# The 96 rows of v around each block, interleaved over the partitions, in a kernel of three stages

## The chip, the cores and the metric

The kernel runs on one core of a Trainium2 chip. The time is device microseconds of one execution from start to end; a median of several executions is given, and the rows come from one profiled execution. Engines are PE (TensorE: matmuls and transposes), DVE (VectorE), ACT (ScalarE), POOL (GpSimd) and SP, whose queue issues nearly all the transfers. PEld is PE's loading of weights, which runs beside its matmuls.

## What is computed

Three stages follow each other, on 2 batches of 768 positions: an attention of 8 heads of 64 in a local window with summary keys, a convolution that gates a product, and a spatial gate. Every input comes as 64-bit floats.

```python
k_sum = k.reshape(B, H, nb, 32, D).max(axis=3)          # 24 summary keys
v_sum = v.reshape(B, H, nb, 32, D).mean(axis=3)
mask_l = np.abs(pos[:, None] - pos[None, :]) < 16       # local window
a = softmax(concat([where(mask_l, q @ k.T / 8, -1e9), q @ k_sum.T / 8 + log(32)]))
x = (a @ concat([v, v_sum]))                            # heads side by side: 768 x 512
gate = sigmoid(causal 5-tap convolution of x);  x = (gate * (x @ w_val)) @ w_out
h = relu(x @ w_in);  u, v = halves of h;  v_n = normalise v over its 512 columns
y = (u * (w_spatial @ v_n + b_spatial)) @ w_out2
```

## The kernel before, in words

The kernel first records every operation, and a class `Planner` then puts them in an order for each engine (`plan`): it keeps a clock for each engine, takes the durations from `cost`, and among the operations that could start picks the one of highest priority. `issue` (line 229; 230 after) hands them to the engines, so that nearly all rows of the profile bear this one line, and the names of tiles and the shapes tell them apart. Priorities come from the string `ORDER`: it lists pieces ("lk" loads one pair's k, "lq" q, "lv" v; "kw" builds the key window; "score", "at" and "pv" are the scores of one tick, their transposes and the product with v; "wout", "in1", "in0", "wval" load a 128-row tile of a weight; "wp" is part of the product of w_out and w_in; "vsum" and "put" are the mean of v; "gate", "val0", "u0" and so on are the later stages). A piece that needs another steps that one first.

The batches and heads form 8 pairs of heads, and 16 ticks of scores (half a sequence of one pair each). The sequence is cut into 12 blocks of 64. For each block the keys that count are 96 rows (the 64 of the block, 16 to the left and 16 to the right, the "halos") and 24 summary rows: 120 in all, which is the partition dimension of the pv product. For v these are partitions 0 to 119 of a tile `VW` of 1536 elements (two heads, 12 blocks, 64 columns), loaded by `load_v`: the 64 block rows into partitions 32 to 95, the left and right halos into the even and odd partitions of 0 to 31, from the neighbouring columns of the same array. Those are three transfers of 384, 96 and 96 KB for each pair. `put_vsum` puts the means into partitions 96 to 119 (a transfer at_u<-at_u for four pairs, and a POOL copy for each).

The keys stand in the same order along the free dimension of `KWT` (built by `windows`: an ACT copy "kev" of the block rows, POOL copies "halo" and "ksum"), and `load_masks` builds the additive mask in that order on POOL, once. In `scores` PE multiplies q with the key window (64x120 matmuls), DVE adds the mask and takes the maximum, ACT takes the exponential, POOL divides. `a_T` transposes on PE (128x128, with the identity in `moves`), and `pv` multiplies (120x64). ACT then splits x into a high part and a rest (`xl`), and the 128x384 matmuls of the later stages can begin.

Weights come as pairs of 32-bit words; `load64` makes one float of them with one ACT and two DVE operations. `w_product` multiplies the two weights between the stages (32 matmuls of 128x512). "hot" is a 128x264 filler matmul on `moves`. The SP queue is one list of transfers in the planned order.

Of the kernel before, what the change touches and what calls it, by code (L numbers as in the profile page):

```python
# [12 lines left out]
ALU = mybir.AluOpType  # L13
# [29 lines left out]
LOOK = {"PE": 0, "ACT": 0, "DVE": 0, "POOL": 100, "SP": 200}  # L43

ORDER = """
    mask hot*2 mask hot in1 wout*2 in1 lk*2 in1 kw hot lq hot wout score hot in1 lk kw wp*2 lq in0*2 wout kw lq
    score lk wp kw wp in0*2 vsum score wval lv lq at cw vsum at lv put score pv wval put lv wp score lv wp at score
    put*2 score wval lq pv score at wval wp hot lk pv at wv wp pv gate val0 at lq wu at pv kw val0 at wu lv wu
    val0*2 wu score wv pv lq lk pv kw pv lk lq score u0 lv u0 lk vsum gate val0 kw val0*3 u0 lv kw wv*2 vsum at put
    score put score*2 lv score*3 u0 put v0*3 at*3 put pv*4 at v0 f0 at ws at u0 v0 at pv*3 gate pv v0 u0 gate val1*2  # L50
    ws val1*4 f0 v1*2 s0 f0 val1*2 v1 s0 v1 u1 f0 f1 v1 s0 v1 u1 f1 u1 ws s0 s1 u1 f0*2 ws s0*2 s1 f1*3 s1 u0 ws*2
    u0 u1 ws s0 s1 s0 s1*2 u1*2 out2*2 u1 f0 s1 out2 s0*3 s1 s0 out2 r*2 s0*2 s1 f1 s1*2 r f1 r*3 s1 r s1 r*2 s1 r*3
"""

WIN = 10240 / 3
# [9 lines left out]
class Planner:  # L65
# [94 lines left out]
    def cost(o, eng, method, args, kw, ins, outs):  # L160
# [14 lines left out]
        if method == "dma_start":  # L175
            run = 4 * min(outs[0].ap[-1][1], ins[0].ap[-1][1]) if ins else 512
            total = 4 * size(outs[0]) * outs[0].ap[0][1]
            parts = outs[0].ap[0][1]
            o.rate = next(k for k in range(16, 0, -1) if parts % k == 0)
            rate = 130 if run <= 512 else 405 if parts > 96 else 235 if parts > 64 else 260 if parts > 16 else 150  # L180
            return (600 if eng == "POOL" else 980 if parts < 32 and run <= 512 else 840 if len(outs[0].ap) > 2 else 600 if parts == 64 else 410), None, total / rate, False
        if eng == "ACT":
            ptr = sum(1 for k in ("bias", "scale") if hasattr(kw.get(k), "ap")) + (method == "mul" and hasattr(args[2], "ap"))
# [265 lines left out]
def tile_kernel(ctx, tc, q, k, v, vn, w_val, conv_w, w_out, w_in, w_sp, b_sp, w_out2, mask_l, mask_r, eye, out):  # L449
# [4 lines left out]
    NB = S // QB  # L454
# [76 lines left out]
    def load_masks():  # L531
        pool.memset(moves, 0.0)
        pool.affine_select(out=moves, in_=moves, pattern=[[-1, 264]], compare_op=ALU.not_equal, fill=1.0, base=112, channel_multiplier=1)
        yield

        a3 = [x.rearrange("p (i c) -> p i c", c=KW) for x in added]
        pool.memset(a3[0][:, :, :WK], 0.0)
        pool.memset(a3[0][:, :, WK:], 27.725887222397812)
        for c in range(2):
            x = a3[0][64 * c : 64 * c + 64]  # L540

            for y, n, key in ((x[:, :, 32:WK], QB, 0), (x[:, :, 0:32:2], 16, -16), (x[:, :, 1:32:2], 16, QB)):
# [72 lines left out]
    def windows(n):  # L615

        need("lk", n + 1)
        kp = KT_[n]
        kw = KWT[n] = unit(F32)[:, : NB * KW].rearrange("p (j c) -> p j c", c=KW)
        km = smalls([P, 1, NS], "km", f"km{n}")  # L620
        dve.tensor_reduce(km[:, 0], kp.rearrange("p (m r) -> p m r", r=32), axis=AX.X, op=ALU.max)
        copy("kev", kw[:, :, 32:WK], kp.rearrange("p (j r) -> p j r", r=QB))

        pool.memset(bass.AP(kw.tensor, kw.offset, [kw.ap[0], [(NB - 1) * KW + 1, 2], [2, 16]]), 0.0)
        for x, y, m, dx, dy in ((QB - 16, KW, NB - 2, [80, 2], [1, 2]), (QB, 1, 2, [(NB - 2) * QB - 16, 1], [(NB - 1) * KW - 1, 1])):
            src = bass.AP(kp.tensor, kp.offset + x, [kp.ap[0], [QB if m > 2 else dx[0], m], dx, [1, 16]])
# [747 lines left out]
```

## Time and profile before

| what | us |
|---|---|
| median of 3 runs | 264.13 (263.94 to 265.03) |
| the profiled execution: its time | 265.06 |
| its span, first to last instruction | 263.3 |
| PE busy | 253.2 (96%) |
| PE weight loads busy | 217.5 (83%) |
| DVE busy | 189.4 (72%) |
| POOL busy | 163.7 (62%) |
| ACT busy | 158.9 (60%) |
| moved by DMA | 31.80 MB, mean 121 GB/s |

The shares are means over the span. The stages differ: the weights, q, k and v come in during the first 60 us, and the products fill the rest.

### The profile page before, as it was taken

The numbers are of one execution on the slowest core, as the hardware profiler recorded it, in microseconds if no ns is written. First come the engines' busy times: TensorE is split into PE (matmuls) and PEld (weight loads), VectorE is DVE, ScalarE is ACT, GpSimd is POOL, SyncE is SP. The second block draws the span as 40 slices with busy tenths as digits, with TensorE's granted clock in tenths as the row PEclk, the third lists the DMA queues.
The fourth block names the chain that finished last, engine by engine and source line by source line (L and its number), as shares of the span: only waits on it lengthen the run. The fifth ranks groups of instructions, "written<-read, shape, count | busy, mean of one in ns | idle before, by whom it ended". The sixth has DMA issues, their size and how long they took to land.

```text
span 263.3 us, 5380 instructions
## 1 busy us (share of the span) xinstructions
PE 253.2 (96%) x1878; PEld 217.5 (83%) x1878; DVE 189.4 (72%) x558; ACT 158.9 (60%) x440; POOL 163.7 (62%) x189
## 2 busy tenths in 40 slices
PE   7799999889999999999999999999999999999995
PEld 5255557459999998988998988999999998888884
DVE  1777969689999997799998687969734485650110
ACT  2578797999998699987453143314647443253222
POOL 7224444799797918991468354526999978863110
PEclk9999999999999999999999999999999999999999
DMA  6999999899730202700000000000000800014213
GB/s 219 404 402 410 312 301 236 238 313 343 258 110 0 92 4 94 276 0 2 2 1 1 0 2 0 0 0 2 1 1 2 319 0 2 0 76 163 80 42 120
DMA packets 10651, 31.80 MB, mean 121 GB/s; under 512 B 1520, under 2 KB 1984, under 8 KB 10624
## 3 DMA queue, kind: packets, MB, share of 16 engines
q1 hardware_dynamic: 10592, 31.43, 35.2%
q8 instruction: 15, 0.25, 0.4%
q14 instruction: 12, 0.10, 0.1%
q0 software_dynamic: 32, 0.02, 0.0%
HBM read 28.20 MB, written 3.15 MB: 119 GB/s over the span
## 4 chain that ended last, share of the span: by engine, by line
PE 75%; DMA 15%; ACT 6%; DVE 2%; SPq 1%; issue 0%; ACTq 0%; DVEq 0%
PE at_ps L229 75%; DMA at_u<-in_moe_w_val_dram 8%; ACT at_u L229 5%; DMA at_u<-in_moe_w_in_dram 4%; DMA at_u<-in_k_dram 3%; DVE at_u L229 1%; ACT at_ps L229 1%; SPq L229 1%; DVE sm L229 0%; ACT xl L229 0%; ACTq L229 0%; DVEq L229 0%
## 5 line engine op out<-in xcount | busy, mean ns | idle before, releaser
L229 PE MATMUL at_ps<-at_u,at_u 128*128 128x384 f32 (+4 forms) x1760 | 234.5, 321 | 3.5 <-DVE at_u L229 1.7
L229 PEld LDWEIGHTS at_ps<-at_u,at_u 128*128 128x128 f32 (+2 forms) x1760 | 201.2, 187 | 33.4 <-issue 14.0
L229 POOL TENSOR_TENSOR at_u<-at_u,at_u 128x384 fp32r<-128x384 f32 (+2 forms) x83 | 103.7, 1271 | 50.5 <-ACT at_u L229 50.0
L229 ACT CAST at_u<-at_u 128x384 fp32r<-128x384 f32 (+2 forms) x83 | 46.4, 593 | 44.0 <-DVE at_u L229 35.4
L229 DVE TENSOR_TENSOR at_u<-at_ps,at_u 128x384 f32<-128x384 f32 (+1 forms) x36 | 19.8, 553 | 36.1 <-PE at_ps L229 34.3
L229 ACT COPY at_u<-at_ps 120x384 f32<-120x384 f32 (+3 forms) x61 | 28.4, 503 | 22.5 <-PE at_ps L229 22.3
L229 ACT ACTIVATE at_u<-at_u,nm 128x120 f32<-128x120 f32 x96 | 36.6, 387 | 2.6 <-DVE nm L229 2.5
L229 POOL TENSOR_TENSOR at_u<-at_u,sm 128x360 f32<-128x360 f32 x32 | 25.6, 827 | 17.3 <-DVE sm L229 12.2
L229 DVE SCALAR_TENSOR_TENSOR at_u<-at_ps,cw,at_u 128x384 f32<-128x384 f32 (+3 forms) x64 | 36.4, 605 | 0.0
L229 DVE CUSTOM_DVE_ANT_0 at_u<-at_ps,mask 128x120 f32<-128x120 f32 x96 | 21.7, 273 | 2.9 <-PE at_ps L229 2.9
L229 ACT ACTIVATE at_ps<-at_u 128x512 f32<-128x512 f32 x20 | 12.9, 647 | 13.6 <-DMA at_u<-in_moe_w_out_dram 6.6
L229 DVE TENSOR_TENSOR at_u<-at_u,at_u 128x256 f32<-128x256 f32 (+2 forms) x25 | 19.1, 769 | 1.5 <-DMA at_u<-in_vn_dram 1.4
L229 ACT ACTIVATE at_u<-at_ps 128x512 f32<-128x512 f32 x20 | 11.5, 598 | 14.1 <-PE at_ps L229 14.1
L229 POOL COPY at_u<-at_u 128x320 f32<-128x320 f32 (+2 forms) x24 | 17.8, 751 | 1.4 <-DMA at_u<-at_u 0.7
L229 ACT ACTIVATION_READ_ACCUMULATOR at_u<-at_u,nm 128x1 f32 x96 | 18.5, 192 | 0.0
L229 DVE TENSOR_TENSOR at_u<-at_u 128x384 f32<-128x384 f32 (+5 forms) x31 | 15.4, 498 | 2.6 <-PE at_ps L229 2.4
L229 DVE TENSOR_SCALAR at_u<-at_u 128x512 uint32<-128x512 uint32 (+1 forms) x21 | 12.2, 581 | 5.4 <-DMA at_u<-in_moe_w_in_dram 5.4
L229 DVE SCALAR_TENSOR_TENSOR at_u<-at_ps,at_u 128x512 uint32<-128x512 uint32 x20 | 13.8, 689 | 2.2 <-ACT at_ps L229 1.1
L229 PE MATMUL at_ps<-moves,at_u 128*120 128x128 f32 x96 | 13.3, 275 | 0.9 <-POOL at_u L229 0.9
L229 PEld LDWEIGHTS at_ps<-moves,at_u 128*120 128x120 f32 x96 | 11.0, 137 | 3.2 <-POOL at_u L229 1.1
L229 DVE SCALAR_TENSOR_TENSOR at_u<-at_u,at_u 128x384 f32<-128x384 f32 x16 | 12.3, 790 | 0.1
L229 POOL TENSOR_TENSOR va<-va,power 128x1 f32<-128x1 f32 x12 | 8.0, 677 | 5.8 <-DVE va L229 5.6
(38 smaller groups left out, 128.4 us busy)
## 6 DMA issues: line engine op xcount, KB each, us to landing
at_u<-in_moe_w_in_dram SPq DMA_DIRECT2D x8, 512.0 KB, 9.0
at_u<-in_moe_w_out_dram SPq DMA_DIRECT2D x8, 512.0 KB
at_u<-in_k_dram SPq DMA_DIRECT2D x8, 384.0 KB, 7.7
at_u<-in_q_dram SPq DMA_DIRECT2D x8, 384.0 KB
at_u<-in_vn_dram SPq DMA_DIRECT2D x6, 512.0 KB, 9.6
at_u<-in_v_dram SPq DMA_DIRECT2D x8, 384.0 KB, 10.7
out_dram<-at_u SPq DMA_DIRECT2D x11, 256.0 KB, 2.0
at_u<-in_moe_w_spatial_dram SPq DMA_DIRECT2D x6, 384.0 KB, 5.9
```

The source lines that it names most:

```text
L229: getattr(real, method)(*[home(x) for x in args], **{k: home(x) for k, x in kw.items()})
```

## The change

The rows of a window stand in another order in the 96 partitions. Of every three partitions, the second and third take two neighbouring rows of the block, and the first takes a halo row, left and right in turn. So each of the three transfers of a pair writes 32 partitions at stride 3, from the first to the last of the 96, 192 KB each; the bytes are the same. The key window and the mask follow the same order. The planner's rate for a transfer of 17 to 64 partitions goes from 260 to 395, and `ORDER` is another string with the same pieces.

```diff
@@ ORDER (the first row of twelve in both)
-    mask hot*2 mask hot in1 wout*2 in1 lk*2 in1 kw hot lq hot wout score hot in1 lk kw wp*2 lq in0*2 wout kw lq
+    mask hot mask hot in1 hot wout*2 lk lq kw in1 lk in1 kw hot wp hot wout hot score hot lq in1 lk score wout in0
...
@@ Planner.cost
-            rate = 130 if run <= 512 else 405 if parts > 96 else 235 if parts > 64 else 260 if parts > 16 else 150
+            rate = 130 if run <= 512 else 405 if parts > 96 else 235 if parts > 64 else 395 if parts > 16 else 150
@@ load_masks
-            for y, n, key in ((x[:, :, 32:WK], QB, 0), (x[:, :, 0:32:2], 16, -16), (x[:, :, 1:32:2], 16, QB)):
-                if key <= 0:
-                    pool.affine_select(out=y, in_=y, pattern=[[0, NI], [1, n]], compare_op=ALU.is_gt, fill=-1e9, base=16 + key, channel_multiplier=-1)
+            for y, n, inc, key in ((x[:, :, 1:WK:3], 32, 2, 0), (x[:, :, 2:WK:3], 32, 2, 1), (x[:, :, 0:WK:6], 16, 1, -16), (x[:, :, 3:WK:6], 16, 1, QB)):
+                if key < QB:
+                    pool.affine_select(out=y, in_=y, pattern=[[0, NI], [inc, n]], compare_op=ALU.is_gt, fill=-1e9, base=16 + key, channel_multiplier=-1)
...
-        pool.memset(a3[0][0:64, 0, 0:32:2], -1e9)
+        pool.memset(a3[0][0:64, 0, 0:WK:6], -1e9)
...
@@ windows
-        copy("kev", kw[:, :, 32:WK], kp.rearrange("p (j r) -> p j r", r=QB))
+        mid = bass.AP(kw.tensor, kw.offset + 1, [kw.ap[0], [KW, NB], [3, QB // 2], [1, 2]])
+        copy("kev", mid, kp.rearrange("p (j i t) -> p j i t", j=NB, t=2))
...
-            dst = bass.AP(kw.tensor, kw.offset + y, [kw.ap[0], [KW if m > 2 else dy[0], m], dy, [2, 16]])
+            dst = bass.AP(kw.tensor, kw.offset + y, [kw.ap[0], [KW if m > 2 else dy[0], m], dy, [6, 16]])
@@ load_v
-        sp.dma_start(dst[32:WK], src)
 
         n = 2 * NB * D
-        for t, at in ((0, 48 * n - D), (1, D)):
-            sp.dma_start(dst[t:32:2], bass.AP(src.tensor, src.offset + at, [[n, 16], [1, n]]))
+        for t in range(2):
+            sp.dma_start(dst[1 + t : WK : 3], bass.AP(src.tensor, src.offset + t * n, [[2 * n, 32], [1, n]]))
+
+        sp.dma_start(dst[0:WK:3], bass.AP(src.tensor, src.offset + 48 * n - D, [[n, 16], [2 * D - 48 * n, 2], [1, n]]))
```

What the planner makes of it is shown at three places. SP's queue from the first w_val tile to the second (the names in_... are the arrays). Before:

```order
L229 DMA at_u_162_897<-in_moe_w_val_dram 128x1024
L229 DMA at_u_166_912<-in_v_dram 64x1536
L229 DMA at_u_166_912<-in_v_dram 16x1536 x2
L229 DMA at_u_131_816<-in_q_dram 128x768
L229 DMA at_u_173_963<-in_vn_dram 128x1024
L229 DMA at_u_174_979<-in_vn_dram 128x1024
L229 DMA at_u_179_994<-in_v_dram 64x1536
L229 DMA at_u_179_994<-in_v_dram 16x1536 x2
L229 DMA at_u_192_1032<-in_moe_w_val_dram 128x1024
```

After, from the vn tiles that stand at the same number of bytes to the second w_val tile:

```order
L230 DMA at_u_163_896<-in_vn_dram 128x1024
L230 DMA at_u_164_910<-in_vn_dram 128x1024
L230 DMA at_u_166_919<-in_v_dram 32x1536
L230 DMA at_u_136_818<-in_q_dram 128x768
L230 DMA at_u_175_943<-in_vn_dram 128x1024
L230 DMA at_u_176_956<-in_vn_dram 128x1024
L230 DMA at_u_186_973<-in_moe_w_in_dram 128x1024
L230 DMA at_u_192_990<-in_v_dram 32x1536
L230 DMA at_u_200_1012<-in_v_dram 32x1536
L230 DMA at_u_208_1024<-in_moe_w_val_dram 128x1024
```

The v transfers of a pair stood together, in front of a q and of the vn tiles; now one third stands at a time, with q, vn and weights in between, and the first pair's other thirds come further down.

PE's rows up to and just behind the first pv product (64x64 rows, whose second operand is a v tile). Before:

```order
L229 MATMUL at_ps_250_1223<-at_u_85_800,at_u_76_766 128x512 x2
L229 MATMUL at_ps_250_1223<-at_u_126_937,at_u_76_766 128x512
L229 MATMUL at_ps_250_1223<-at_u_85_800,at_u_126_937 128x512
L229 MATMUL at_ps_252_1247<-moves 128x264
L229 MATMUL at_ps_257_1267<-moves,at_u_160_955 120x128 x3
L229 MATMUL at_ps_259_1273<-moves,at_u_160_955 120x128 x3
L229 MATMUL at_ps_263_1279<-at_u_85_800,at_u_76_766 128x512 x2
L229 MATMUL at_ps_263_1279<-at_u_126_937,at_u_76_766 128x512
L229 MATMUL at_ps_263_1279<-at_u_85_800,at_u_126_937 128x512
L229 MATMUL at_ps_188_1292<-at_u_169_1017,at_u_166_912 64x64 x12
L229 MATMUL at_ps_270_1308<-moves,at_u_186_1088 120x128 x3
L229 MATMUL at_ps_232_1315<-at_u_169_1017,at_u_179_994 64x64 x12
```

After:

```order
L230 MATMUL at_ps_233_1213<-at_u_93_862,at_u_75_765 128x512
L230 MATMUL at_ps_233_1213<-at_u_141_994,at_u_75_765 128x512
L230 MATMUL at_ps_233_1213<-at_u_75_765,at_u_93_862 128x512
L230 MATMUL at_ps_233_1213<-at_u_172_1039,at_u_93_862 128x512
L230 MATMUL at_ps_229_1236<-at_u_146_940,at_u_166_919 64x64 x12
L230 MATMUL at_ps_238_1251<-moves,at_u_161_1005 120x128
L230 MATMUL at_ps_235_1255<-at_u_146_940,at_u_192_990 64x64 x12
L230 MATMUL at_ps_238_1251<-moves,at_u_161_1005 120x128 x2
L230 MATMUL at_ps_240_1279<-moves,at_u_161_1005 120x128 x3
L230 MATMUL at_ps_242_1284<-at_u_167_987,at_u_136_818 64x120 x2
L230 MATMUL at_ps_243_1290<-at_u_167_987,at_u_136_818 64x120 x2
L230 MATMUL at_ps_242_1284<-at_u_167_987,at_u_136_818 64x120 x2
```

The filler (128x264) and transposes (120x128) that stood ahead of the first pv product are gone from there; transposes and a tick of scores (64x120) stand behind it.

DVE's rows at the first convolutions (SCALAR_TENSOR_TENSOR with cw) and the eighth tick's masked scores (ISA with mask). Before, from the second half of that tick's last masked score:

```order
L229 ISA nm_237 128x1
L229 TENSOR_SCALAR sm_224<-sums_223 128x6
L229 RECIPROCAL sm_224<-sm_224 128x6
L229 TENSOR_SCALAR at_u_227_1125<-at_u_227_1125 128x512
L229 SCALAR_TENSOR_TENSOR at_u_227_1125<-at_ps_228_1255,at_u_227_1125 128x512
L229 TENSOR_SCALAR sm_239<-sums_238 128x6
L229 RECIPROCAL sm_239<-sm_239 128x6
L229 TENSOR_REDUCE km_285<-at_u_253_1243 128x24
L229 TENSOR_SCALAR at_u_246_1239<-at_u_246_1239 128x512
L229 SCALAR_TENSOR_TENSOR at_u_246_1239<-at_ps_247_1285,at_u_246_1239 128x512
L229 TENSOR_TENSOR at_u_189_1319<-at_ps_188_1292,at_u_189_1319 128x384
L229 SCALAR_TENSOR_TENSOR at_u_191_1330<-at_ps_188_1292,cw,at_u_191_1330 128x383
```

After:

```order
L230 SCALAR_TENSOR_TENSOR at_u_232_1264<-at_ps_229_1236,cw,at_u_232_1264 128x380
L230 SCALAR_TENSOR_TENSOR at_u_232_1264<-at_ps_235_1255,cw,at_u_232_1264 128x383
L230 ISA at_u_217_1180,nm_244<-at_ps_242_1284,mask_69 128x120
L230 ISA nm_244 128x1
L230 SCALAR_TENSOR_TENSOR at_u_232_1264<-at_ps_235_1255,cw,at_u_232_1264 128x382
L230 ISA at_u_217_1180,nm_244<-at_ps_242_1284,mask_69 128x120
L230 ISA nm_244 128x1
L230 SCALAR_TENSOR_TENSOR at_u_232_1264<-at_ps_235_1255,cw,at_u_232_1264 128x381
L230 ISA at_u_217_1180,nm_244<-at_ps_242_1284,mask_69 128x120
L230 ISA nm_244 128x1
```

The masked scores of the eighth tick stood ahead of the first convolution; they stand between its taps now.

## Rows read from the trace of the kernel before

**Rows 1.** Busy time by stretch: us, engines (instructions), granted clock, DMA share, GB/s.

```profile
0.00:60.00 60.00, 53.31 (x412) 31.71 (x414) 44.35 (x167) 46.63 (x153) 31.85 (x60) 1.00 0.96 316
60.00:100.00 40.00, 40.00 (x461) 38.38 (x458) 39.93 (x148) 35.90 (x119) 29.86 (x40) 1.00 0.38 125
100.00:260.00 160.00, 159.61 (x1013) 147.38 (x1011) 105.11 (x246) 76.05 (x170) 101.95 (x91) 1.00 0.13 47
```

**Rows 2.** PE's timeline, 0 to 60 us: start, length, work, idle time before and releaser.

```profile
12.30 3.00 PE L229 MATMUL at_ps<-at_u,at_u 128*128 128x512 f32 x28 [1.19 <-DVE at_u L229]
...
25.83 3.70 PE L229 MATMUL at_ps<-at_u,at_u 128*128 128x512 f32 x8 [0.53 <-DVE at_u L229]
29.37 1.47 PE L229 MATMUL at_ps<-moves,at_u 128*120 128x128 f32 x12
...
35.95 4.72 PE L229 MATMUL at_ps<-at_u,at_u 64*64 64x120 f32 x32 [0.66 <-DMA at_u<-in_q_dram]
...
41.25 2.71 PE L229 MATMUL at_ps<-at_u,at_u 64*64 64x120 f32 x72
...
48.17 0.61 PE L229 MATMUL at_ps<-moves 128*128 128x264 f32 x2
...
49.99 0.55 PE L229 MATMUL at_ps<-moves,at_u 128*120 128x128 f32 x3 [0.89 <-POOL at_u L229]
...
55.23 0.92 PE L229 MATMUL at_ps<-at_u,at_u 120*64 120x64 f32 x24
56.93 0.62 PE L229 MATMUL at_ps<-at_u,at_u 128*128 128x384 f32 x2 [0.79 <-ACT xl L229]
```

**Rows 3.** The chain that ended last, two pieces of it: start, length, what.

```profile
34.76 9.55 DMA at_u<-in_moe_w_val_dram
...
56.95 156.70 PE at_ps L229 x1291
```

**Rows 4.** Busy time in stretches of the front, columns as in rows 1.

```profile
0.00:28.00 28.00, 23.64 (x113) 13.04 (x114) 18.18 (x64) 17.31 (x45) 12.44 (x39) 1.00 0.94 361
10.00:28.00 18.00, 16.29 (x98) 8.29 (x97) 14.58 (x57) 13.45 (x41) 7.42 (x18) 1.00 1.02 408
28.00:50.00 22.00, 20.46 (x178) 12.52 (x176) 17.53 (x90) 19.32 (x76) 10.14 (x14) 1.00 1.00 264
...
54.00:56.00 2.00, 2.00 (x51) 1.76 (x51) 1.76 (x2) 2.00 (x6) 2.00 (x2) 1.00 0.98 395
56.00:58.00 2.00, 1.22 (x12) 0.84 (x8) 1.90 (x4) 2.00 (x8) 1.99 (x2) 1.00 1.00 207
...
74.00:76.00 2.00, 2.00 (x12) 1.94 (x13) 2.00 (x13) 2.00 (x12) 2.00 (x3) 1.00 0.47 160
```

**Rows 5.** SP's timeline of transfers issued: start, length of the issues, what.

```profile
22.29 2.47 SPq L229 DMA_DIRECT2D at_u<-in_v_dram  x3
...
35.37 6.81 SPq L229 DMA_DIRECT2D at_u<-in_v_dram  x6
...
51.65 1.84 SPq L229 DMA_DIRECT2D at_u<-in_v_dram  x3
...
70.82 1.75 SPq L229 DMA_DIRECT2D at_u<-in_vn_dram  x2
```

**Rows 6.** Groups by form: count, busy us, mean ns, idle before.

```profile
L229 DVE CUSTOM_DVE_ANT_0 at_u<-at_ps,mask 128x120 f32<-128x120 f32 x96 | 21.7, 273 | 2.9 <-PE at_ps L229 2.9
...
L229 ACT COPY at_u<-at_u 128x768 f32<-128x768 f32 x8 | 6.7, 835 | 0.8 <-DMA at_u<-in_k_dram 0.8
L229 POOL COPY at_u<-at_u 128x320 f32<-128x320 f32 x8 | 4.4, 544 | 0.3
L229 POOL COPY at_u<-km 128x288 f32<-128x288 f32 x8 | 3.4, 429 | 0.3
...
L229 POOL TENSOR_SCALAR_AFFINE_SELECT mask<-mask 64x192 f32<-64x192 f32 x4 | 1.4, 352 | 0.2
L229 POOL MEMSET at_u<- 128x32 f32 x8 | 1.0, 130 | 12.2 <-ACT at_u L229 12.2
```

More of the change, by code (lines that the diff above doesn't have):

```diff
@@ L45 @@
 ORDER = """
-    mask hot*2 mask hot in1 wout*2 in1 lk*2 in1 kw hot lq hot wout score hot in1 lk kw wp*2 lq in0*2 wout kw lq
[L47 to L52, printed above, removed]
+    mask hot mask hot in1 hot wout*2 lk lq kw in1 lk in1 kw hot wp hot wout hot score hot lq in1 lk score wout in0
+    kw lq wval in0 lk at in0 wp at score vsum lv kw lq wp*2 cw vsum put score in0 wp wu lv score lv put score put
+    wval score wp lq wval lv wp pv put wp pv at score at*2 lk at pv wu pv gate at wval val0*2 pv at kw pv val0*2
+    score lk wu wv score pv*2 kw wu u0 gate vsum*2 lq lk u0*2 val0 at kw u0 score wv lv*2 put lq put score lk kw wv
+    score wv lq score*2 lv score val0*3 at v0 at v0 at lv v0 at pv*3 v0 u0 v0 at*2 f0 at pv put pv ws put pv out2 ws
+    pv*2 u0 v0 u0 gate val1 gate val1*2 s0 u0 val1*3 v1 val1 v1 ws v1 val1 u1 v1*2 f1 s0 u1 f0 u1 v1 f1 u1*3 s0 out2
+    s0 s1 u1 s1 ws f0*3 s1 s0 f1 ws*2 s0 s1 u1 s0 s1 out2 s0*2 f1 f0 s0 out2 s1 s0 ws s1 s0 f0 r s0*2 f1 r s1 r s1
+    f1 s1*3 f1 s1*2 r*9
 """
@@ L540, in load_masks @@
             x = a3[0][64 * c : 64 * c + 64]
-            for y, n, key in ((x[:, :, 32:WK], QB, 0), (x[:, :, 0:32:2], 16, -16), (x[:, :, 1:32:2], 16, QB)):
-                if key <= 0:
-                    pool.affine_select(out=y, in_=y, pattern=[[0, NI], [1, n]], compare_op=ALU.is_gt, fill=-1e9, base=16 + key, channel_multiplier=-1)
+            for y, n, inc, key in ((x[:, :, 1:WK:3], 32, 2, 0), (x[:, :, 2:WK:3], 32, 2, 1), (x[:, :, 0:WK:6], 16, 1, -16), (x[:, :, 3:WK:6], 16, 1, QB)):
+                if key < QB:
+                    pool.affine_select(out=y, in_=y, pattern=[[0, NI], [inc, n]], compare_op=ALU.is_gt, fill=-1e9, base=16 + key, channel_multiplier=-1)
                 if key >= 0:
-                    pool.affine_select(out=y, in_=y, pattern=[[0, NI], [-1, n]], compare_op=ALU.is_gt, fill=-1e9, base=16 - key, channel_multiplier=1)
+                    pool.affine_select(out=y, in_=y, pattern=[[0, NI], [-inc, n]], compare_op=ALU.is_gt, fill=-1e9, base=16 - key, channel_multiplier=1)
         pool.tensor_copy(added[1], added[0])
-        pool.memset(a3[0][0:64, 0, 0:32:2], -1e9)
-        pool.memset(a3[1][64:128, NI - 1, 1:32:2], -1e9)
+        pool.memset(a3[0][0:64, 0, 0:WK:6], -1e9)
+        pool.memset(a3[1][64:128, NI - 1, 3:WK:6], -1e9)
         yield
@@ L621, in windows @@
         dve.tensor_reduce(km[:, 0], kp.rearrange("p (m r) -> p m r", r=32), axis=AX.X, op=ALU.max)
-        copy("kev", kw[:, :, 32:WK], kp.rearrange("p (j r) -> p j r", r=QB))
-        pool.memset(bass.AP(kw.tensor, kw.offset, [kw.ap[0], [(NB - 1) * KW + 1, 2], [2, 16]]), 0.0)
-        for x, y, m, dx, dy in ((QB - 16, KW, NB - 2, [80, 2], [1, 2]), (QB, 1, 2, [(NB - 2) * QB - 16, 1], [(NB - 1) * KW - 1, 1])):
+        mid = bass.AP(kw.tensor, kw.offset + 1, [kw.ap[0], [KW, NB], [3, QB // 2], [1, 2]])
+        copy("kev", mid, kp.rearrange("p (j i t) -> p j i t", j=NB, t=2))
+        pool.memset(bass.AP(kw.tensor, kw.offset, [kw.ap[0], [(NB - 1) * KW + 3, 2], [6, 16]]), 0.0)
+        for x, y, m, dx, dy in ((QB - 16, KW, NB - 2, [80, 2], [3, 2]), (QB, 3, 2, [(NB - 2) * QB - 16, 1], [(NB - 1) * KW - 3, 1])):
             src = bass.AP(kp.tensor, kp.offset + x, [kp.ap[0], [QB if m > 2 else dx[0], m], dx, [1, 16]])
-            dst = bass.AP(kw.tensor, kw.offset + y, [kw.ap[0], [KW if m > 2 else dy[0], m], dy, [2, 16]])
+            dst = bass.AP(kw.tensor, kw.offset + y, [kw.ap[0], [KW if m > 2 else dy[0], m], dy, [6, 16]])
             copy("halo", dst, src)
```

## The prediction

> **What bounds the kernel now.** I read first the table of busy time by stretch. From 60 us on TensorE (PE) has no room: 40.00 of 40.00 us busy up to 100, 159.61 of 160 up to 260 [rows 1]. [...] Before 60 us PE is busy for 53.31 us and idle for 6.69, while the DMA share is 0.96 [rows 1].
>
> Second I read PE's own timeline for the places of that idle time [rows 2]. One is early, 1.19 us for a w_in tile that DVE rebuilds. Four lie later: 0.53 us (DVE, the fourth w_out tile), 0.66 (a q transfer), 0.89 (POOL: normalised scores for the transposes), 0.79 (ACT: the low part of x, just before the first 128x384 product). The four sum to 2.87 us; what is left of the 6.69, 2.63, lies in the first microseconds, before any weight has arrived. A filler matmul, 0.61 us at 48.17, stands between them.
>
> Third, the chain that ended last: it goes through the second w_val transfer, issued at 34.76 and landed 9.55 later, and becomes PE for good at 56.95 [rows 3]; ACT, between the two, is busy for 19.32 of the 22 us up to 50 [rows 4]. So in the front PE waits for what DMA and ACT bring late.
>
> Fourth, what DMA moves in the front [rows 4]. Both stretches have all 16 engines busy, but 10 to 28 us moves 408 GB/s and 28 to 50 us only 264. The second is where the window loads of the first four pairs (576 KB or 0.59 MB each, 2.36 MB in all) land: their twelve transfers are issued between 22.29 and 42.18 [rows 5], behind what is still queued. 22 us at 264 GB/s are 5.81 MB; the other 3.45 MB at 408 would take 8.5 us, which leaves 13.5 us for the four pairs, 3.4 us each or 175 GB/s. A later pair, issued at 51.65 [rows 5], shows its parts: 395 GB/s from 54 to 56 us (64 rows), 207 from 56 to 58 (16-row halos), both at a share near 1 [rows 4].
>
> **The change part by part.** (a) The window loads. The trace has no transfer of 32 rows at stride 3. The nearest that spans 96 partitions is the pair of vn transfers issued at 70.82 [rows 5]: 160 GB/s at a share of 0.47 from 74 to 76 us [rows 4], that is 340 GB/s at full share. Bounds: 408 (as 128 rows) gives 1.45 us a pair, 175 (as the pairs now) 3.4. I take 333, a little under the vn pair: 1.77 us a pair.
>
> When does the last byte land that the first pv product needs? The mean of v (put) is the last, and in both queues 15,488 KB or 15.86 MB stand ahead of it (in the new one the first pair's last third is the transfer just before). 361 GB/s up to 28 us are 10.11 MB [rows 4], so 5.75 MB follow; the old queue reaches them at 28 + 5.75 / 0.264 = 49.8 us, and the first pv runs at 55.23 [rows 2], 5.4 later. In the new queue those 5.75 MB hold eight thirds (1.57 MB): at 333 they take 4.7 us, the other 4.18 MB at 408 take 10.2, and the mean's turn comes at 28 + 14.9 = 43. With the same 5.4 us behind it the first pv is fed at about 48.4.
>
> (b) The order of pieces. PE reaches its first pv product with less behind it: before it stand 12 transposes instead of 30, at 1.47 / 12 = 0.12 us each [rows 2] 2.2 us less, and one score tick fewer (24 of the trace's records, at 2.71 / 72 [rows 2] 0.9 us). What waits there: the fourth w_out tile has 1,024 KB less ahead (2.6 us at 408 GB/s), against a wait of 0.53; the second q of its unit stands behind one third of a pair instead of a whole one, and 0.66 us ends there; the transposes for which PE waited 0.89 us for POOL stand behind the first pv; and between the first pv and the first 128x384 product stand a score tick and some thirty transposes, which cover the 0.79 us. So PE is at the first pv at about 55.2 - 0.9 - 2.2 - 2.1 (the waits ahead of it) = 50.0, and what feeds it is there 1.6 us before. I take 2.3 of the 2.87 us as removed, because a wait of half a microsecond is likely to show up somewhere in an order as tight as this one. Bounds: 0 and 2.87.
>
> (c) The start. The filler of 0.61 us leaves the middle for the front, where PE waits for weights anyway. The second w_in tile of the product moves from SP place 4 to 6, 768 KB or 1.9 us later; its old wait is 1.19 us, and now score ticks and fillers stand ahead of it. I put the sum of both at a gain of 0.2: the bounds are a gain of 0.6 (the filler goes, nothing else changes) and a loss of 0.6 (twice that is lost to the later tile).
>
> (d) The copies into the key window and the masks. The key copy on ACT (835 ns, 8 times) and POOL's halo copies write at other strides with the same element counts [rows 6]. POOL's halo copy writes every second element now, at 544 ns for 320, or 1.70 ns an element, against 429 for 288 in a copy that writes runs, 1.49. So a stride costs at most about 14%, and those two differ in their reads too: 8 x 0.12 us on ACT at most. I take 0; four of the eight would lie in the front. For the masks four selects of 64x192 (352 ns) become eight of half the size, at most 1.4 us more on POOL, and POOL later waits 12.2 us for ACT ahead of the key window's memsets [rows 6], so 0. Were that cover gone, the first scores would be late by 1.4 us.
>
> **Sum:** 2.3 + 0.2 + 0 + 0 = 2.5 us off the profiled execution: 265.06 - 2.5 = 262.6, its span 260.8. That execution lies 0.93 us above the median of the three runs, so against the median: 264.13 - 2.5 = **261.6 us**.
>
> **Rivals.** *All idle time of the front that can go goes:* the four waits (2.87), the 1.19, the filler (0.61) and 0.39 in the back: 5.06 us, so 264.13 - 5.06 = 259.1 at the far end. For it speaks that what feeds the first pv is 1.6 us ahead of PE; against it that ACT is 46.63 us busy in the first 60 and 19.32 of 22 from 28 to 50 [rows 1, 4], so work brought earlier meets an engine nearly full.
>
> *The loads are no faster.* By the two parts seen alone, 0.39 MB at 395 and 0.20 MB at 207 [rows 4], the old pair takes 1.00 + 0.95 = 1.95 us, hardly more than 1.77; the 3.4 us of the mean may come from the company that the pairs keep. If the thirds too come at 175 GB/s, their 1.57 MB take 9.0 us and the mean's turn comes at 28 + 19.2 = 47.2, four later than above. The first pv is then fed at 52.6, while PE is there at 50.0: the hole of 2.6 us takes back what (b) wins. The time is 264.1 - 2.5 + 2.6 = 264.2 then. [...]
>
> *Slower: DVE becomes the bound.* DVE is busy for 39.93 of 40 us from 60 to 100 [rows 1], side by side with PE. Six masked score instructions of 273 ns [rows 6], 1.64 us, stood ahead of the first convolutions and stand between them now. If the first convolutions don't start earlier by as much, gates and values come 1.64 us later, PE waits for them, and what PE won in the front is waited away: 264.13 + 1.6 = 265.8. It decides when DVE's 15.65 us of idle time in the first 60 stay as they are; if they shrink by 1.64, this rival is gone. Against it speaks that DVE gets its inputs (vn, w_val) earlier by the new queue.
>
> **How the numbers follow.** No change means within 0.5%, about what a measurement of this kernel can tell from none: 262.8 to 265.4. My forecast (260.6 to 262.8) has a chance of 0.48; all the idle time (under 260.6) 0.16; loads no faster (262.8 to 265.4) 0.21; DVE as the bound (over 265.4) 0.15. That gives faster 0.64, same 0.21, slower 0.15. The range leaves out the slower case and a few in a hundred below: 259.5 to 265.3. The likeliest case's own range is 260.6 to 262.8.
>
> **What would show it.** In the changed profile: the stretch 28 to 50 us (or to where the first four pairs are in) at 330 GB/s or more rather than 264, at a share of 1; PE busy for about 55.8 of the first 60 us; the first 120x64 matmuls at about 50 to 52 us, not 55.23; no 128x384 product that waits for ACT. The forecast is wrong if a wait for a v transfer or for the mean stands in front of the first pv, if DVE shows up as the releaser of PE between 60 and 100 us, or if PE's idle time after 60 grows past its present half microsecond.

## The result, and the profile after

The changed kernel takes 267.93 us (median of 4 runs, 267.16 to 272.78) against 264.53 for the kernel before in the same comparison: a ratio of 1.012, 95% interval 1.0077 to 1.0162. (Every ratio here is one of means; the run of 272.78 was in a slower state of the chip and is not in it.) The change makes the kernel slower by 1.2%; the forecast was 261.6, faster by 1%. The profiled execution took 267.54 us, its span 265.8.

Busy time by stretch after the change, to be laid beside [rows 1], then the stretch of [rows 4] and four short ones (columns as there):

```profile
0.00:60.00 60.00, 52.05 (x387) 31.29 (x388) 41.42 (x159) 45.35 (x142) 34.44 (x64) 0.97 0.96 322
60.00:100.00 40.00, 39.06 (x470) 36.92 (x470) 38.48 (x164) 37.14 (x133) 30.18 (x40) 1.00 0.40 116
100.00:260.00 160.00, 159.93 (x1004) 147.51 (x1003) 104.61 (x237) 74.79 (x166) 102.45 (x91) 1.00 0.13 46
28.00:50.00 22.00, 18.45 (x130) 9.19 (x128) 16.18 (x82) 18.52 (x74) 8.00 (x12) 1.00 0.97 285
48.00:50.00 2.00, 0.00 (x0) 0.00 (x0) 1.50 (x6) 0.71 (x2) 0.66 (x1) 1.00 0.74 223
50.00:52.00 2.00, 1.14 (x24) 1.06 (x24) 0.00 (x0) 0.00 (x0) 2.00 (x2) 0.81 0.90 214
52.00:54.00 2.00, 2.00 (x29) 1.62 (x27) 0.79 (x2) 1.85 (x5) 1.86 (x4) 0.50 0.90 309
54.00:56.00 2.00, 2.00 (x30) 1.71 (x30) 1.08 (x3) 2.00 (x6) 1.92 (x2) 0.83 0.99 300
```

PE is idle for 7.95 us of the first 60 (6.69 before) and for 0.94 of the next 40, where it had no idle time before. From 48 to 50 us it does nothing at all, and in the 6 us behind that its granted clock is 0.81, 0.50 and 0.83. PE's timeline has the places (columns as in [rows 2]):

```profile
8.12 3.70 PE L230 MATMUL at_ps<-at_u 128*128 128x512 f32 x8 [1.49 <-DVE at_u L230]
...
13.84 1.12 PE L230 MATMUL at_ps<-at_u 128*128 128x512 f32 x2 [0.18 <-DVE at_u L230]
...
31.54 8.14 PE L230 MATMUL at_ps<-at_u,at_u 64*64 64x120 f32 x106 [0.37 <-DMA at_u<-in_q_dram]
39.86 7.13 PE L230 MATMUL at_ps<-at_u,at_u 128*128 128x512 f32 x16 [0.18 <-DVE at_u L230]
50.86 1.25 PE L230 MATMUL at_ps<-at_u,at_u 120*64 120x64 f32 x24 [3.86 <-POOL at_u L230]
...
65.29 1.57 PE L230 MATMUL at_ps<-at_u,at_u 120*64 120x64 f32 x8 [0.86 <-issue]
```

The waits that the new order was to end are nearly gone: 0.53, 0.66, 0.89 and 0.79 us [rows 2] have become 0.37 and 0.18. One wait of 3.86 us stands in their place, right in front of the first pv product. PE arrives there at 39.86 + 7.13 = 46.99 us, 8 us earlier than before, and has nothing to multiply. The chain says what it waits for (columns as in [rows 3]):

```profile
32.83 10.68 DMA at_u<-in_moe_w_val_dram
...
43.52 5.67 DMA at_u<-at_u
...
49.34 1.47 POOL at_u L230
...
50.86 9.64 PE at_ps L230 x126
```

It is the mean of v: its transfer (at_u<-at_u) is issued once an older one on the queue has landed (a w_val tile, at 43.51), lands 5.67 us later, at 49.2, and is copied by POOL. POOL's timeline has the copies, here and then in the kernel before (columns as for PE):

```profile
49.34 2.87 POOL L230 COPY at_u<-at_u 24x1536 f32<-24x1536 f32 x2 [3.84 <-DMA at_u<-at_u]
52.08 5.91 POOL L229 COPY at_u<-at_u 24x1536 f32<-24x1536 f32 x4 [0.65 <-DMA at_u<-at_u]
```

DVE's timeline shows a second late transfer at the same place, k, for whose reductions DVE stands still in its own order, ahead of the convolution's taps (the instructions that add up its five steps):

```profile
47.04 0.95 DVE L230 TENSOR_REDUCE km<-at_u 128x24 f32<-128x768 f32 x1 [4.50 <-DMA at_u<-in_k_dram]
...
55.82 0.95 DVE L230 TENSOR_REDUCE km<-at_u 128x24 f32<-128x768 f32 x1 [0.88 <-DMA at_u<-in_k_dram]
```

### The profile page after: what moved, and what is told of

It reads as the page before. It is cut to its first block, busy times and chain, and to the rows that moved or that the text cites. A ratio compares the mean times of both kernels' runs of the same rounds, so it can differ in the third digit from the quotient of the medians.

```text
span 265.8 us, 5374 instructions
## 1 busy us (share of the span) xinstructions
PE 253.8 (95%) x1878; PEld 218.2 (82%) x1878; DVE 184.5 (69%) x558; ACT 158.5 (60%) x440; POOL 167.1 (63%) x193
## 4 chain that ended last, share of the span: by engine, by line
PE 80%; DMA 17%; SPq 1%; issue 1%; POOL 1%; ACT 0%; DVE 0%; POOLq 0%
PE at_ps L230 80%; DMA at_u<-in_q_dram 7%; DMA at_u<-in_moe_w_val_dram 4%; DMA at_u<-in_k_dram 3%; DMA at_u<-at_u 2%; SPq L230 1%; POOL at_u L230 1%; ACT at_u L230 0%; DVE at_u L230 0%; POOLq L230 0%
## 5 line engine op out<-in xcount | busy, mean ns | idle before, releaser
L230 PE MATMUL at_ps<-at_u,at_u 128*128 128x384 f32 (+4 forms) x1744 | 228.0, 321 | 5.4 <-POOL at_u L230 3.9
L230 PEld LDWEIGHTS at_ps<-at_u,at_u 128*128 128x128 f32 (+2 forms) x1744 | 199.0, 188 | 31.8 <-issue 12.3
L230 ACT CAST at_u<-at_u 128x384 fp32r<-128x384 f32 (+2 forms) x83 | 45.7, 590 | 42.3 <-DVE at_u L230 21.6
L230 POOL COPY at_u<-at_u 128x320 f32<-128x320 f32 (+2 forms) x24 | 21.1, 882 | 7.6 <-DMA at_u<-at_u 3.8
L230 DVE TENSOR_TENSOR at_u<-at_u 128x384 f32<-128x384 f32 (+5 forms) x31 | 16.8, 549 | 2.4 <-PE at_ps L230 2.4
L230 DVE TENSOR_TENSOR at_u<-at_u,at_u 128x256 f32<-128x256 f32 (+2 forms) x25 | 16.5, 664 | 0.5 <-DMA at_u<-in_vn_dram 0.4
L230 DVE TENSOR_SCALAR at_u<-at_u 128x512 uint32<-128x512 uint32 (+1 forms) x21 | 10.0, 479 | 5.5 <-DMA at_u<-in_moe_w_in_dram 5.4
L230 DVE BATCH_NORM_STATS2 st<-at_u 128x6 f32<-128x512 f32 x12 | 8.3, 691 | 7.6 <-ACT at_u L230 7.5
```

What stands on the lines that cost most here:

```text
L230: getattr(real, method)(*[home(x) for x in args], **{k: home(x) for k, x in kw.items()})
```

## The experiments

In all of them the planner's order was written out as a list and played back, instruction for instruction, so that a change of rows or of one queue moves nothing else; the rate measurements add transfers behind that list. Code and lists are shown shortened.

```diff
-        order, real_ = self.plan(), {}
+        seq, place = json.loads(...)   # the list of one kernel
+        order, real_ = [self.ops[i] for i in seq], {}
```

**New order, old rows.** `load_v`, `windows` and the mask as before the change, in the order of the changed kernel.

> The order of the changed kernel, instruction for instruction, with the rows of v, the key window and the mask of the kernel before: the 64 block rows take the place of the first third of a pair, each 16 halo rows that of a later third. The masks keep eight selects. Theory 1 (the rows don't matter; the packets of v take 333 ns in the new rows and 341 in the old): 267 to 269 us, with the wait in front of the first pv between 3 and 5 us. Theory 2 (the new rows load more slowly in this company and make the mean late): about 264, the wait under 1 us. Theory 3 (the new rows are faster, and only the order is bad): 269.5 or more, the wait 5 us or more.

Measured: 267.07 us, ratio 1.0078 (1.0048 to 1.0109) to the kernel before. The loss is 0.8% without the new rows. PE's waits and DVE's:

```profile
49.12 0.92 PE L331 MATMUL at_ps<-at_u,at_u 120*64 120x64 f32 x24 [0.64 <-POOL at_u L331]
...
58.71 0.84 PE L331 MATMUL at_ps<-moves,at_u 128*120 128x128 f32 x6 [2.42 <-DVE at_u L331]
```

```profile
56.11 0.95 DVE L331 TENSOR_REDUCE km<-at_u 128x24 f32<-128x768 f32 x1 [2.91 <-DMA at_u<-in_k_dram]
```

No theory holds as a whole: the time is in theory 1's range, the wait for the mean (0.64 instead of 3.86 us) in theory 2's. Of the 3.2 us by which that wait shrank 1.7 are the mean's, since the first pv starts at 49.12 and not at 50.86; the rest is PE coming later, in an execution whose granted clock was low from 8 to 14 us (see the part on the clock). That the old rows load faster in this order shows more directly in what was moved. Up to 28 us both kernels moved the same, 363 and 362 GB/s; then, in the order old rows, new rows, old rows, old rows:

```profile
28.00:42.00 14.00, 13.79 (x137) 7.60 (x131) 13.87 (x72) 13.45 (x56) 5.94 (x10) 1.00 1.02 382
28.00:42.00 14.00, 13.45 (x119) 7.29 (x118) 13.19 (x73) 11.81 (x53) 5.19 (x9) 1.00 1.03 311
42.00:47.00 5.00, 5.00 (x13) 2.16 (x12) 2.46 (x15) 5.00 (x21) 2.83 (x3) 1.00 0.67 172
47.00:50.00 3.00, 2.36 (x29) 1.20 (x27) 2.93 (x6) 2.11 (x5) 2.40 (x2) 1.00 0.47 122
```

At a full share the old rows move 382 GB/s and the new ones 311. The head start does not reach the second k. From 42 to 50 us the share is 0.67 and 0.47: SP comes to the second k only at 49.56, behind the four small transfers of the mean (12 KB each) and behind the landing of the first k at 46.49, so that it lands at 56.1; with the new rows it landed at 55.8. The chain that ended last has both (columns as in [rows 3]):

```profile
36.77 9.72 DMA at_u<-in_k_dram
...
49.56 6.52 DMA at_u<-in_k_dram
```

This is read from the trace; no run was made for it. DVE stands 2.91 us for that k, and PE 2.42 us behind DVE. No theory had that.

**Old order, new rows.**

> The order of the kernel before, with the interleaved rows in v, the key window and the mask (the only added instructions are four selects of the mask). Theory 1 (the rows don't matter): within 0.5% of the kernel before, 263.5 to 265.5. Theory 2 (the new rows load more slowly): 266 or more. Theory 3 (they load faster; then the mean and the second w_val tile land earlier, and the waits of 0.66 and 0.89 us go): 262.5 to 263.

Measured: 265.96 us, 1.004 (1.0015 to 1.0065). From 28 to 50 us:

```profile
28.00:50.00 22.00, 20.00 (x173) 11.97 (x172) 17.43 (x89) 17.32 (x66) 8.67 (x11) 1.00 1.03 258
```

The time lies between the ranges of theories 1 and 2. 258 GB/s against 264 [rows 4], at a full share, is a small difference, but on the side of theory 2, as 311 against 382 is; a gain by the rows themselves, which my prediction rested on, is out. The 0.4% are not the loads' alone, since this run also has the slower copies into the key window and four more selects. The two halves of the change, 0.4% and 0.8%, add up to its 1.2% within their intervals.

**The mean early, on SP's queue alone.**

```diff
 SP, from the first pair's second third on
-w_val, v3, bias, k, v1, v2, v0 (last third), mean, v1, v2, ...
+v0 (last third), w_val, v3, k, mean, v1, v1, v2, v2, bias, ...
```

> The changed kernel with another sequence on the SP queue alone: the last third of the first pair moves up behind the second, and the transfer of the mean moves from behind 15,488 KB to behind 14,720 KB; the spatial bias and five thirds of pairs 1 and 2 stand behind it. Theory 1 (the 3.86 us of PE in front of the first pv are a wait for the mean, and they cost the clock as well): the mean lands at 45 to 46.5 instead of 49.2, the wait is under 1.5 us, the clock stays nearer to 1, and the time falls by 2.5 to 4.5 us, to 263.5 to 265.5. Rival (something else is late at the same place: ACT, POOL, or the next v): the wait moves to the next product and the time stays at 267 to 268.

Measured: 269.34 us, 1.0176 (1.0136 to 1.0215). The wait for the mean shrank as the theory said, but the rival's mechanism held: the wait moved. The time is above the rival's range too.

```profile
48.74 0.92 PE L331 MATMUL at_ps<-at_u,at_u 120*64 120x64 f32 x24 [0.95 <-POOL at_u L331]
...
59.99 0.84 PE L331 MATMUL at_ps<-moves,at_u 128*120 128x128 f32 x6 [3.34 <-DVE at_u L331]
```

```profile
57.38 0.95 DVE L331 TENSOR_REDUCE km<-at_u 128x24 f32<-128x768 f32 x1 [3.69 <-DMA at_u<-in_k_dram]
```

The wait of 3.86 us is 0.95, and 3.34 us come back eleven microseconds later, behind DVE's wait for k.

**Fillers in the gap.**

```diff
+    for i in range(6):
+        awake(7 + i)
```

In the list that is played back the six stand on PE ahead of the first pv product.

> The changed kernel with six more filler matmuls of 128x264 on PE in front of the first pv product, in a PSUM bank that nothing else holds there, so that PE is busy while it waits for the mean. Theory 1 (part of the loss is the granted clock, 0.81, 0.50 and 0.83 in the three stretches of 2 us from 50 to 56 us after PE stood idle): the clock stays at 1.00 there, the first pv starts at the same 50.9 us, and the time falls by 0.6 to 1.5 us. Rival (PE had room there, so the clock costs nothing): no change, 267 to 268.5; or longer, if the fillers last beyond the wait.

Measured: 273.4 us, 1.0329 (1.0276 to 1.0382). A miss:

```profile
51.44 6.68 PE L334 MATMUL at_ps<-moves 128*128 128x264 f32 x12 [3.14 <-DVE at_u L334]
```

The fillers themselves wait 3.14 us for DVE, which still reads their bank for a w_val tile behind its wait for the first k; the bank was not free, as the expectation had it. It is another bank than that of the first pv product, so the run tells nothing of what held that product. The fillers ran behind the gap instead of in it, at a low granted clock (0.72, 0.50, 0.50 and 0.57 from 52 to 60 us), and what the clock costs stayed untested here.

**Half the bytes of v, in both orders.** Each v transfer carries the first head of its pair alone, and the second head's product reads the first head's rows.

```diff
-            sp.dma_start(dst[1 + t : WK : 3], bass.AP(src.tensor, src.offset + t * n, [[2 * n, 32], [1, n]]))
+            sp.dma_start(dst[1 + t : WK : 3, :m], bass.AP(src.tensor, src.offset + t * n, [[2 * n, 32], [1, m]]))   # m = n // 2
...
-                        vw[0:KW, h, 2 * NI * g + jj, :],
+                        vw[0:KW, 0, 2 * NI * g + jj, :],
```

> The changed kernel, instruction for instruction, with half the bytes in each v transfer (the first head of each pair alone; the product for the second head reads the first head's rows, so half of v is left out). The transfers then take about as long as whole ones would at twice their rate. Theory 1 (late transfers are the whole loss of the new order): the wait in front of the first pv falls under 1 us, DVE's waits for k shrink, and the time falls to 261 to 264 us. Rival (the new order loses by itself, by ACT or DVE): 266 or more.

> The kernel before, instruction for instruction, with half the bytes in each v transfer, as in the run beside it. Theory 1: the four waits of 2.87 us in all shrink to 1 us or less, 262 to 263.5 us; the new order with the same help is then faster than the old one by up to 1.5 us. Rival (the old order is bound by ACT in the front, not by transfers): 264 to 264.6, no change.

Measured: new order 264.44 us, 1.001 (0.9985 to 1.0034); old order 262.81, 0.9929 (0.9902 to 0.9957). By the ratios, fewer bytes are worth about 2.9 us to the new order and 1.9 to the old one, and the new order is not the better one even then: with half the bytes DVE still waits for the second k.

```profile
54.05 0.95 DVE L331 TENSOR_REDUCE km<-at_u 128x24 f32<-128x768 f32 x1 [2.10 <-DMA at_u<-in_k_dram]
```

**k and the mean early, on SP's queue alone.**

```diff
 SP, from the first pair's second third on
+v0 (last third), w_val, k, v3, mean, v1, v1, k (second), v2, v2, v3, w_val, v3, bias, ...
```

> The changed kernel with another sequence on the SP queue alone: the first pair's last third and the mean early, as in the run that did only this and lost the gain to DVE's wait for k (3.69 us at 57.4 us), and the second k of that unit moved up by 1.4 MB, ahead of the last w_val tile, the fourth pair's thirds, the third pair's thirds and the spatial bias. Theory 1 (in front of the first convolutions DVE's order holds two reductions of k, and their transfers are late): DVE's wait there falls under 1 us, PE's under 1.5 us, and the time falls to 264 to 266. Rival (what is moved back is late instead: w_val or v of pairs 3 and 4): 267 to 270.

Measured: 264.44 us, 0.9992 (0.9959 to 1.0025): with the new rows, the new order on every other engine, and all its bytes, the loss is gone; the forecast gain has not come. PE's largest waits behind the start, and DVE's:

```profile
50.02 0.92 PE L331 MATMUL at_ps<-at_u,at_u 120*64 120x64 f32 x24 [1.56 <-POOL at_u L331]
...
63.38 1.57 PE L331 MATMUL at_ps<-at_u,at_u 120*64 120x64 f32 x9 [0.81 <-issue]
```

```profile
47.53 0.95 DVE L331 TENSOR_REDUCE km<-at_u 128x24 f32<-128x768 f32 x1 [3.19 <-DMA at_u<-in_k_dram]
```

The wait for the second k is gone and so is PE's behind it; 1.56 us for the mean stay, a little over the 1.5 expected.

**Rates by themselves.** Sets of transfers behind the last result, nothing else running; POOL reads each of a set's four pairs when it has landed, so that the distance of two reads is the time of a pair. "In company" is with other transfers queued between the parts.

> The kernel before, with seven sets of transfers behind its last result, each set alone on the queue and each of four pairs of heads, 2.36 MB: the three old parts of a pair; the three new thirds; the 64 block rows alone (partitions 32 to 95); 32 rows in partitions 0 to 31; 32 rows in 64 to 95; 32 rows at stride 4 over all 128; and 128 rows. From the first runs (packets of 6 KB took 382 ns on an engine in the new rows and 341 in the old ones under the same order of instructions) theory 1, the stride itself slows the new thirds: new thirds at 200 to 270 GB/s, the old parts at 290 to 330. [...] Theory 3, my prediction: new thirds at 333 or more. Rows in 0 to 31 alone, and in 64 to 95 alone, about 207; block rows 395; 128 rows 408.

Of this run only the first two sets count, 3.0 us a pair for the old parts and 2.2 for the new thirds; in most of the others one transfer wrote over the rows of the last, and waited for it (three of 32 rows took 6.2 us). It was made again:

> The kernel before, with eight sets of transfers behind its last result, each of four pairs: the three old parts of a pair; the three new thirds; the 64 block rows and both halos in one transfer of 32 rows; the 96 rows in one transfer (of other data); 128 rows; and the first three again with a transfer of 128 rows (384 KB) behind each part, as in the front of the kernel. Theory 1 (a transfer's pattern alone sets its rate): the pair takes 3.0, 2.2, 2.1 us alone, as the first measurement gave for the first two, and the new thirds save 0.8 us a pair in company too. Theory 2 (the old parts leave room that a neighbour fills, the new thirds leave none, as packets of 341 and 382 ns under the same order say): in company the new thirds take as long as the old parts or longer.

POOL's reads: old parts alone, new thirds alone, 128 rows (0.79 MB a read), then old parts and new thirds with 128 rows behind each part:

```profile
266.81 0.18 POOL L332 COPY keep<-at_u 96x4 f32<-96x4 f32 x1 [12.02 <-DMA at_u<-in_v_dram]
...
274.88 0.18 POOL L332 COPY keep<-at_u 96x4 f32<-96x4 f32 x1 [2.69 <-DMA at_u<-in_v_dram]
276.71 0.18 POOL L332 COPY keep<-at_u 96x4 f32<-96x4 f32 x1 [1.64 <-DMA at_u<-in_v_dram]
...
283.07 0.18 POOL L332 COPY keep<-at_u 96x4 f32<-96x4 f32 x1 [1.84 <-DMA at_u<-in_v_dram]
...
303.56 0.19 POOL L332 COPY keep<-at_u 128x4 f32<-128x4 f32 x1 [0.82 <-DMA at_u<-in_q_dram]
...
309.42 0.19 POOL L332 COPY keep<-at_u 128x4 f32<-128x4 f32 x1 [1.75 <-DMA at_u<-in_q_dram]
314.93 0.18 POOL L332 COPY keep<-at_u 96x4 f32<-96x4 f32 x1 [5.32 <-DMA at_u<-in_v_dram]
...
331.18 0.90 POOL L332 COPY keep<-at_u 96x4 f32<-96x4 f32 x7 [5.42 <-DMA at_u<-in_v_dram]
338.87 0.19 POOL L332 COPY keep<-at_u 96x4 f32<-96x4 f32 x1 [6.79 <-DMA at_u<-in_v_dram]
...
358.20 0.90 POOL L332 COPY keep<-at_u 96x4 f32<-96x4 f32 x7 [6.25 <-DMA at_u<-in_v_dram]
```

Between the first and the last read of a set lie three pairs of heads. Alone: (274.88 - 266.81) / 3 = 2.69 us for the old parts, (283.07 - 276.71) / 3 = 2.12 for the new thirds; 128 rows take 1.95 us for 0.79 MB, 403 GB/s. With 128 rows behind each part (1.18 MB a pair, 2.93 us at that rate): 5.42 for the old, 6.44 for the new, which leaves, as an estimate, 2.49 us for an old pair and 3.51 for a new one. So the thirds are the faster pair alone and the slower one in company, by 1.0 us (6.44 - 5.42): theory 2. This is one execution, with four pairs a set; that the kernel's own streams differ the same way (311 against 382 GB/s) bears it out. In the changed kernel's front the loads of v have company of this kind: between thirds at 31.42, 34.12 and 38.12 us SP issues a w_val tile (32.83), the bias (36.36) and a k (37.31). (Both halos in one transfer: 2.53 alone, 4.67 - 1.95 = 2.72 in company.)

**Two versions that might have beaten both.** The old kernel with both halos in one transfer, and the new order with old rows, both halos in one transfer, and k and the mean early.

```diff
-        for t, at in ((0, 48 * n - D), (1, D)):
-            sp.dma_start(dst[t:32:2], bass.AP(src.tensor, src.offset + at, [[n, 16], [1, n]]))
+        sp.dma_start(dst[0:32], bass.AP(src.tensor, src.offset + 48 * n - D, [[n, 16], [2 * D - 48 * n, 2], [1, n]]))
```

> The kernel before, instruction for instruction, with the left and right halos of a pair in one transfer of 32 rows (partitions 0 to 31) in the first halo's place on the queue; the second halo's transfer is gone. If the two transfers of 16 rows are what is slow in a pair (3.0 us alone, of which the 64 rows take 1.0): the transfers of the front land up to 3 us earlier and the time falls by 0.5 to 1.3 us, the gain that half the bytes gave (262.8). Rival (in company the halos cost no time of their own): no change.

> The changed kernel's order with the SP sequence that moves k and the mean up, with the old rows, the halos in one transfer. Theory (the new order loses by late transfers only): the time is at or under that of the same sequence with the new rows (264.4), 262.5 to 264.5, and the wait in front of the first pv is under 1.6 us. Rival (the new order loses by its own DVE and ACT programs): 264.5 or more.

Measured: 264.77 us, 1.0018 (0.9991 to 1.0045), no change; and 264.07, 0.9998 (0.9968 to 1.0028), no change. In the second, PE is idle for only 4.50 us of the first 60, against 6.69 before, and still nothing is won: its granted clock is 0.97 there and 0.96 in the next 40 us.

```profile
0.00:60.00 60.00, 55.50 (x446) 33.40 (x448) 48.10 (x171) 48.39 (x157) 35.09 (x67) 0.97 0.96 334
60.00:100.00 40.00, 38.20 (x426) 36.55 (x422) 36.27 (x156) 35.33 (x126) 27.55 (x37) 0.96 0.34 99
```

PE's last wait in the front is one for which the profile names no releaser. I read it as a wait for DVE's taps, which would hold that product's bank; this is not shown, but the next run bears on it:

```profile
62.57 1.77 PE L331 MATMUL at_ps<-at_u,at_u 120*64 120x64 f32 x8 [1.73 <-issue]
```

To end it, the reductions of k and the eighth tick's masked scores were moved behind the taps on DVE:

> The kernel with the new order, the old rows with halos in one transfer and k and the mean moved up on SP (264.07 before), with another sequence on DVE alone: the two reductions of k and the eighth tick's six masked scores stand behind the convolution taps of the first two pairs instead of among them. Theory (what is left of the new order's loss is that the taps of the first pairs finish late on DVE, since the bank of a later pv product is theirs: PE waits 1.73 us at 62.6): that wait falls under 0.7 us and the time falls by 0.7 to 1.5 us, to 262.6 to 263.4, faster than both kernels. Rival (the scores moved back come late to ACT and POOL): 264 or more.

Measured: 269.34 us, 1.018 (1.0148 to 1.0213). The wait at 62.6 is gone, as it would be if it was for the taps, but the next scores come 3.30 us late, as the rival said. In this run the eighth tick's masked scores are read after their bank has been handed on in program order, so part of them is of other data; only its time is read.

```profile
73.38 1.97 PE L331 MATMUL at_ps<-at_u,at_u 64*64 64x120 f32 x36 [3.30 <-ACT at_u L331]
```

## Why the prediction was wrong

**What held.** What bounds the kernel: PE from 60 us on (busy for 39.06 of 40 us, then for 159.93 of 160), transfers ahead of it (a DMA share of 0.96). The waits that the sum counted went about as counted, too: the four of 2.87 us are 0.55, so 2.32 went, where I took 2.3 without a worked reason, so that the closeness is in part luck; the two at the weights, 0.78 (in the 2.63 of the start) and 1.19, are 1.49 and 0.18, a gain of 0.30 where I took 0.2. But time won ahead of a later wait is no gain. The mask's selects cost POOL 1.1 us (8 of 323 ns, 4 of 352 before), hidden as said. POOL's halo copies were mis-sized: 880 ns and not at most 14% over 544 [rows 6], 2.7 us in all, which is hidden too, since POOL still waits 3.84 us for the mean.

**The step that failed** is (a): "I take 333, a little under the vn pair: 1.77 us a pair". The vn rows were the nearest in partitions, but alone on the queue. Up to 47 us the changed kernel moves

```profile
28.00:47.00 19.00, 18.45 (x130) 9.19 (x128) 13.73 (x75) 16.81 (x71) 7.35 (x11) 1.00 1.03 302
```

so that the 15.86 MB ahead of the mean are through at 47.0 (10.14 MB up to 28 us, 5.74 from there), and not at "28 + 14.9 = 43". With the prediction's own 10.2 us for the other bytes, the eight thirds took 8.8 us: 179 GB/s, 3.3 us a pair, an estimate near the 3.51 worked out above for a pair in company, where an old pair takes 2.49.

Three more steps went wrong behind it. The "same 5.4 us behind it" were taken for the time that feeding needs; but before the change POOL copied the mean from 52.08 on, and PE came to the product at 55.23 without a wait, busy with its own order. Behind the turn at 47.0 feeding took 3.9 us: the first pv was fed at 50.86, 2.5 later than forecast and not 4, an error that by luck took back part of the first. In (b) PE was to be there at 50.0 and was there at 46.99, since the scores and transposes ahead of it took some 5.4 us less, where 3.1 were taken. So the margin of 1.6 us became a hole of 3.86: 2.5 us by the late mean, 3.0 by the early PE. And the waits of DVE's order for two reductions of k ahead of the taps, 4.50 and 0.88 us, stand in no term: the prediction followed one path, from the mean to the first pv. The run with the old rows shows what that leaves out: a loss of 0.8% comes with the new order alone, part of it with a low clock (below).

PE's idle time is 1.9 us more in the span, its busy time 0.6 more. Even where the loss was cured (264.44 with k and the mean early, 264.07 with the old rows as well) the 2.5 us of gain never came. In the profile of the second the granted clock is low (0.97 and 0.96); in that of the first it is 1.00, and why it gains nothing stays open.

**The rivals.** "The loads are no faster" is the mechanism that came about: its turn of 47.2 is the measured 47.0. It got a hole of 2.6 and put the result at 264.2: it let the time end where the gain is eaten up. But PE comes earlier than it had it, and the order that waits for the mean also holds DVE for k. The late k alone is enough for a loss: with the mean 1.7 us earlier (267.07, in part the clock's), or early by its place on the queue (269.34), the time stays long; with k early as well the loss is gone (264.44). A late mean with k early was not tried. The DVE rival's test, its idle time in the first 60 us, came out against me: 18.6 us, not less than 15.65; and its range, over 265.4, holds the measured time. But that is luck: it was not the six masked scores that made DVE late in front of the taps, it was k. "All idle time goes" is out, as idle time grew.

In the kernel the new thirds came at about 179 GB/s and the old pairs at 175, each in its own order, both estimates. Where only the rows differ they are not equal: the new rows move 311 GB/s against 382 under the new order (28 to 42 us) and 258 against 264 under the old one (28 to 50 us), and by themselves the new thirds take 0.8 times the old parts' time alone (2.12 us against 2.69) and 1.4 times in company (3.51 against 2.49, the estimates above). What in the pattern makes that turn was not tried and stays open.

**The clock.** Two stretches with the same products give a price for the low clock. PE's first eight products of 128x512 take 3.70 us at a granted clock of 1.00 and, in the run of the new order with old rows, where the clock was 0.94 over the first 28 us (0.69, 0.50 and 0.96 from 8 to 14), 5.40:

```profile
8.07 5.40 PE L331 MATMUL at_ps<-at_u 128*128 128x512 f32 x8 [2.00 <-DVE at_u L331]
```

From the first pv product to the first 128x384 the changed kernel takes 8.70 us behind its hole (50.86 to 59.56), at 0.81, 0.50 and 0.83 up to 56, and the run with k and the mean early 7.76 (50.02 to 57.78), 0.23 of it a wait, at 1.00:

```profile
59.56 4.88 PE L230 MATMUL at_ps<-at_u,at_u 128*128 128x384 f32 x82
57.78 4.78 PE L331 MATMUL at_ps<-at_u,at_u 128*128 128x384 f32 x81
```

So the low clock costs about 1.7 us in the one and 1.2 in the other, estimates from these differences. A gap does not settle it: the run with the mean early kept 1.00 behind a gap of 3.34 us, and the one with the halos in one transfer fell to 0.50 (64 to 66 us) behind one of 1.73. The timed runs agree with this in part. The new order with old rows took 264.59 and 266.05 us in its two runs at a mean granted clock of 1.000 and 267.3 to 267.9 in the five at 0.986 or 0.987, so a good part of its loss goes with the clock; where in those runs it fell is not on record. With halos in one transfer and k and the mean early, the five runs at 1.000 average 263.5 us, 0.7 under the kernel before at 0.998 and more, and the two at 0.987 took 266.1, where nothing of that gain is left; the five between, at 0.993 and 0.994, took 262.8 to 266.6. With the mean alone early the one run at 1.000 still took 267.84, so the loss behind the late k is not the clock's alone. Why the granted clock falls in one run and not in the next is not shown.

## What to carry to other kernels

Measure a transfer's rate in the company it will keep: here the layout that won alone (2.12 us a pair against 2.69) lost between other transfers (6.44 us against 5.42, with 128 rows behind each part), and the planner, which was given 395 GB/s where about 179 came in the front (an estimate), found an order that counted on bytes it did not have. When waits are removed, ask what stands next in the path and is late by the same cause, here two transfers on one queue: curing one of them moved the wait (3.86 us became 0.95 and, later, 3.34), and curing both ended the loss (264.44 us), though it made no gain. An order searched against a cost model should be read at the first place where an engine waits for a transfer, since what stands behind it in that engine's list came late as well here: PE's first pv product and all behind it after 3.86 us for the mean and, with the old rows, its transposes 2.42 us behind DVE's 2.91 us for k.

## What the hardware showed that I had not expected

A transfer of 32 rows of 6 KB at stride 3 over 96 partitions took 2.12 us for three against 2.69 for the old 64 + 16 + 16, and 6.44 against 5.42 with a transfer of 128 rows behind each (3.51 against 2.49 without those rows, an estimate). PE's granted clock was still 1.00 inside the hole (48 to 50 us), 0.81 from 50 to 52, where PE resumed, and 0.50 only from 52 to 54, with PE busy throughout; behind a hole of 3.34 us in another run it stayed at 1.00.
